# Twelve loads of small weights issued by GpSimd instead of SyncE, in a transformer block's forward and backward pass, with a new written-out order

## The chip, the cores and the metric

The kernel runs on one core of a Trainium2 chip. The metric is the device time of one execution in microseconds (us), as the median of several runs. A core has five engines with a queue of instructions each, and each queue is worked off in order: TensorE (PE; its weight loads are listed apart as PEld), VectorE (DVE), ScalarE (ACT), GpSimd (POOL) and SyncE (SP). SyncE only issues data movements (DMAs); ScalarE and GpSimd can issue them too. An instruction that waits for another engine, or for a DMA to land, holds up everything behind it in its own queue.

## The reference

The inputs are two batches of 4000 tokens with 144 channels, in bf16, and seven small weights. Shortened to what matters:

```python
xa = layernorm(x)
q, k, v = split(xa @ w_qkv)
glob = softmax(q @ k.T * D ** -0.5) @ v @ w_att_out
u, g = split(gelu(xa @ w_mlp_in))
g = layernorm(g)
loc = (u * conv5(g, dw_csgu)) @ w_mlp_out        # 5 taps along the tokens, per channel
m = concat(glob, loc)
out = x + (m + conv5(m, dw_merge)) @ w_merge
```

The kernel must return the output and, for a given grad_out, the gradients of x and of all seven weights.

## The kernel before

Tokens lie on 125 partitions, 32 blocks of 125 tokens to a batch. The body walks over the 64 blocks of both batches. For each block it computes the scores against all 4000 tokens of the batch (`ps`, four pieces of 1000; lines L1187 and L1194), the row minimum of the negated scores (L1209, on VectorE), the exponentials (L1215, on ScalarE, into `Pbuf`), the products for the backward pass (`Sbuf`), transposes of both by DMA (`PT`, `ST`), and the sums over tokens (L1236, L1266, L1322). Pieces of the local branch (the gelu and the convolution) are put between them. A last stage, from about 1000 us on, does the output and the weight gradients.

The head, the first 40 us, prepares this for batch 0. It does the following:

- It loads x in four groups of eight blocks, w_qkv, and the other weights. `Head.loads` (L148 to L163) issues w_qkv from ScalarE and the other twelve loads from SyncE. Each weight of 144 rows takes two loads, rows 0 to 127 (L153) and rows 128 to 143 (L154), into parts of the tile `raw`; `dwt` holds the merge taps (L157); `Wi` and `Wi2` hold w_mlp_in (L161 to L163).
- It computes the layernorm of x by groups: `lnst` (bn_stats on VectorE, L362), a few small steps to the variance `lnve` (L373), the root `rstd_x` (a power, on GpSimd, L374), `lnnm` (L378), then the normalized blocks `xa_aug`, two of a group on ScalarE (L383), four on VectorE (L385), two on GpSimd (L387). TensorE transposes them (L392 and L396), ScalarE copies the result to `xaT_m` (L393) and VectorE to `R` (L397); each group so has one R copy. A PSUM tile that an R copy reads is free for the next transposes only when the copy is done.
- It folds weights together: the q/k product `Q` and part of `RW` (L204, L205), the tap columns `cols` from transposes of `dwt` (L215, L217 to L219), the merge weight scaled by each tap (`sWm`: one half on ScalarE at L238, ten products; the other half on GpSimd at L240, ten products), the product of w_att_out with the value weights (L181) and from these `VUT` (L253, L259). `jit_q` and `jit_b` make the rows `qb` of the first two blocks, which TensorE transposes to `qt` (L1354).
- 36 matmuls on zeros (`warm`, L192) are spread over the head's TensorE queue.

The order within each queue is neither the program's order nor a scheduler's: the class `Planner` holds a table `ORDER` with one list of numbers for each of the five engines, over the whole program, and chains the instructions (on TensorE, runs of matmuls) in that order. The numbers count the instructions of an engine in program order, so a load that moves from one engine to another renumbers both lists.

Of the kernel before, what the change touches and what calls it, by code (L numbers as in the profile page):

```python
# [15 lines left out]
D = 144  # L16
DR = 16
# [103 lines left out]
class Head:  # L121
# [7 lines left out]
    def loads(self):  # L129
# [26 lines left out]
        ld(self.Wo, k.w_att_out, 0, nc.sync)  # L156
        nc.sync.dma_start(self.dwt[:], k.dw_merge)  # L157
        ld(self.Wl, k.w_mlp_out, 0, nc.sync)
        for h in range(2):
            ld(self.Wm[h], k.w_merge, h * D, nc.sync)  # L160
        nc.sync.dma_start(W.Wi[0:128, 0, :], k.w_mlp_in[0:128, :])  # L161
        nc.sync.dma_start(W.Wi[96:96 + DR, 1, :], k.w_mlp_in[128:D, :])
        nc.sync.dma_start(self.Wi2[:], k.w_mlp_in[128:D, :])  # L163
# [612 lines left out]
class Planner:  # L776

    ORDER = {
# [1414 lines left out]
```

## Time and profile before

| what | us |
|---|---|
| median of three runs | 1152.78 (1150.36 to 1153.01) |
| the profiled execution | 1152.39 |
| its span in the trace | 1150.5 |
| TensorE busy | 1118.8 (97%) |
| VectorE busy | 1021.0 (89%) |
| ScalarE busy | 906.5 (79%) |
| GpSimd busy | 249.5 (22%) |

The span runs from the first to the last instruction of the trace; the rest of the profiled execution's time lies around it. Views of the trace that the text uses: *stages* give each engine's busy time in stretches of the span; *waits* name who waited for whom; *the chain of waits* follows the last instruction back, at each step to what released it; *groups* add up the instructions of a line; *the timeline* lists them by start. "PE ps L1187" means an instruction of TensorE at line 1187 that writes the tile `ps`. A busy TensorE is modelled from pipelined matmuls, and the share of one engine over the whole span is a mean of stages with different limits.

### The profile page before, as it was taken

What the parts mean: (1) busy time and instruction counts of PE and PEld (TensorE: products, weight loads), DVE (VectorE), ACT (ScalarE), POOL (GpSimd) and SP (SyncE); (2) the same over time, 40 slices, a digit from 0 to 9 for tenths busy, and PEclk for the clock granted to TensorE, in tenths of its full rate; (3) what the DMA queues carried; (4) which work ended last, traced back from release to release, by engine and by line L of the source; (5) the groups of instructions that cost most, each with busy time, mean ns of one, the idle gap of its engine ahead of it and who ended that gap; (6) DMA issues with size and microseconds to landing.
All of it is one profiled execution on the core that took longest, in us unless ns stands there. A gap on an engine that the chain in (4) does not pass through costs nothing.

```text
span 1150.5 us, 35851 instructions
## 1 busy us (share of the span) xinstructions
PE 1118.8 (97%) x14293; PEld 868.7 (76%) x14293; DVE 1021.0 (89%) x3063; ACT 906.5 (79%) x1641; POOL 249.5 (22%) x427
## 2 busy tenths in 40 slices
PE   6999999999999999999999999999999999999998
PEld 3667777777777677777777777777777777699987
DVE  8699999999999998877999999999999997667656
ACT  5999898899898767777989889888889877615372
POOL 8111112111121113431001111111111112013642
PEclk9999999999999999999999999999999999999999
DMA  4688887979988989998988989888888899978973
GB/s 117 155 160 176 173 181 158 192 159 173 174 166 159 188 181 182 201 187 183 207 183 178 171 158 168 161 181 152 173 174 154 187 177 183 224 173 219 245 144 101
DMA packets 680887, 200.72 MB, mean 174 GB/s; under 512 B 657815, under 2 KB 674093, under 8 KB 680699
## 3 DMA queue, kind: packets, MB, share of 16 engines
q1 hardware_dynamic: 678352, 194.69, 84.6%
q0 software_dynamic: 2192, 3.62, 1.1%
q8 instruction: 111, 1.82, 0.7%
q14 instruction: 56, 0.46, 0.1%
q10 hardware_dynamic: 176, 0.12, 0.0%
HBM read 24.62 MB, written 18.01 MB: 37 GB/s over the span
## 4 chain that ended last, share of the span: by engine, by line
PE 64%; DMA 13%; DVE 11%; ACT 7%; issue 2%; SPq 1%; POOL 1%; ACTq 0%; DVEq 0%; POOLq 0%
PE X L1322 18%; PE ps L1187 14%; PE yz L1236 8%; PE yz L1266 8%; PE ps L1194 5%; DMA PT<-Pbuf 5%; DVE Pbuf L1209 4%; ACT Pbuf L1215 3%; PE po L1708 2%; DMA ST<-Sbuf 2%; PE pd L610 1%; DVE Sbuf L1226 1%; PE pj L1147 1%; ACT Sbuf L1225 1%; DMA go_h<-in_grad_out_dram 1%
## 5 line engine op out<-in xcount | busy, mean ns | idle before, releaser
L1209 DVE TENSOR_SCALAR_CACHE_REDUCE Pbuf<-ps 125x1000 bf16<-125x1000 f32 x256 | 306.2, 1197 | 30.1 <-PE ps L1194 22.4
L1225 ACT CAST Sbuf<-ps 125x1000 bf16<-125x1000 f32 x249 | 248.7, 999 | 86.7 <-PE ps L1194 66.2
L1215 ACT ACTIVATE Pbuf<-Pbuf,nm 125x1000 bf16<-125x1000 bf16 x256 | 284.9, 1144 | 4.4 <-DVE nm L1211 4.2
L1322 PE MATMUL X<-QBs,Pbuf 125*128 125x144 bf16 x2048 | 281.1, 226 | 0.2 <-POOL QBs L1256 0.2
L1322 PE MATMUL X<-QBs,Sbuf 125*128 125x144 bf16 x2048 | 281.3, 226 | 0.0
L1187 PE MATMUL ps<-xaT_m,qt 128*128 128x500 bf16 x1024 | 260.6, 374 | 5.0 <-DVE Pbuf L1209 3.5
L1322 PEld LDWEIGHTS <-Sbuf 125*128 125x128 bf16 x2048 | 198.2, 98 | 18.8 <-issue 18.5
L1322 PEld LDWEIGHTS <-Pbuf 125*128 125x128 bf16 x2048 | 200.2, 98 | 1.3 <-issue 1.1
L1226 DVE TENSOR_TENSOR Sbuf<-Sbuf,Pbuf 125x1024 bf16<-125x1024 bf16 x249 | 170.8, 690 | 7.9 <-ACT Sbuf L1225 6.0
L1236 PE MATMUL yz<-xa_aug,PT 125*128 125x145 bf16 x2048 | 151.0, 227 | 6.5 <-DMA PT<-Pbuf 6.4
L1266 PE MATMUL yz<-xa_aug,ST 125*128 125x144 bf16 x2048 | 150.8, 228 | 3.6 <-DMA ST<-Sbuf 2.4
L1236 PEld LDWEIGHTS <-PT 125*128 125x128 bf16 x2048 | 130.7, 98 | 21.6 <-DMA PT<-Pbuf 10.5
L1187 PEld LDWEIGHTS <-qt 128*128 128x128 bf16 x1024 | 91.4, 97 | 68.6 <-issue 7.0
L1266 PEld LDWEIGHTS <-ST 125*128 125x128 bf16 x2048 | 132.9, 98 | 12.2 <-issue 7.1
L1329 DVE TENSOR_TENSOR acc<-X,acc 125x432 f32<-125x432 f32 (+1 forms) x204 | 109.8, 548 | 15.3 <-PE X L1322 14.8
L1256 POOL TENSOR_TENSOR QBs<-g,g 125x144 bf16<-125x144 f32 x64 | 35.2, 550 | 379.2 <-ACT g L1255 290.9
L1194 PEld LDWEIGHTS <-qt 16*128 16x128 bf16 x1024 | 26.3, 91 | 108.9 <-issue 108.9
L1194 PE MATMUL ps<-XR,qt 16*128 16x500 bf16 x1016 | 100.4, 380 | 0.0
L681 POOL TENSOR_SCALAR l_w<-ring,nc,c 125x144 f32<-125x144 bf16 x64 | 31.8, 504 | 167.0 <-DVE nc L677 122.4
L653 DVE TENSOR_TENSOR l_prod<-ring,Wc 125x720 bf16<-125x720 bf16 x128 | 65.9, 535 | 0.2
L1611 PE MATMUL Hps<-Yg,go_h 125*128 125x144 bf16 x640 | 54.3, 226 | 0.0
L600 POOL TENSOR_TENSOR rsr<-ve,mhalf 125x2 f32<-125x2 f32 x32 | 25.4, 795 | 126.9 <-DVE ve L599 107.4
(540 smaller groups left out, 1946.4 us busy)
## 6 DMA issues: line engine op xcount, KB each, us to landing
Yn_d<-yn SPq DMA_DIRECT2D x64, 36.0 KB
Zn_d<-qb SPq DMA_DIRECT2D x64, 36.0 KB
ug_d<-ugr SPq DMA_DIRECT2D x32, 72.0 KB
Yg<-Yn_d SPq DMA_DIRECT2D x8, 288.0 KB
Yg<-ug_d SPq DMA_DIRECT2D x8, 288.0 KB
Zn<-Zn_d SPq DMA_DIRECT2D x4, 576.0 KB
PT<-Pbuf SPq DMA_TRANSPOSE x128
ST<-Sbuf SPq DMA_TRANSPOSE x128
```

The lines of the kernel that those rows point to most:

```text
L653: nc.vector.tensor_tensor(prod[:, bi].rearrange("p a b -> p (a b)"), ring[:, a, p + bi:p + bi + 5, :].rearrange("p a b -> p (a b)"), W.Wc[ ...
L1187: mm = nc.tensor.matmul(pp[r // 2][:, r % 2, 0:CH], QT[i][:, 2 * h, :], bs(i)[0].xaT_m[:, c * CH:(c + 1) * CH], start=True, stop=False)
L1194: nc.tensor.matmul(pp[r // 2][:, r % 2, 0:CH], QT[i][rs, 2 * h + 1, :], xr, start=False, stop=True)
L1209: nc.vector.tensor_scalar(pv(pc(i, c2)), src, -1.0, 3.0e38, op0=ALU.mult, op1=ALU.min, accum_out=NM[i][:, c2:c2 + 1])
L1215: nc.scalar.activation(v, v, ACT.Exp, bias=NM[i][:, 4:5], scale=-1.0)
L1225: nc.scalar.copy(pv(sc(i, c2)), src)
L1226: nc.vector.tensor_tensor(sc(i, c2), sc(i, c2), pc(i, c2), op=ALU.mult)
L1236: nc.tensor.matmul(Yw, PT[0:PB, pos(i, j), :], S.xa_aug[:, j, 0:D + 1], start=(j == 0), stop=(j == NB - 1))
L1266: nc.tensor.matmul(Zw, ST[0:PB, j, :], S.xa_aug[:, j, 0:D], start=(j == 0), stop=(j == NB - 1))
L1322: nc.tensor.matmul(X[:, jj, :], l, r, start=(n_ == 0), stop=(n_ == len(ops) - 1))
L1329: nc.vector.tensor_tensor(av, X[0:PB, 0:nj, :], av, op=ALU.add)
L1611: nc.tensor.matmul(H[0:rows, a // 3, (a % 3) * D:(a % 3 + 1) * D], lhs, self.src[b][h][:, 2 + j, :], start=(n == 0 and a % 3 == 0), stop=( ...
```

## The change

The twelve loads other than w_qkv are issued by GpSimd. In the program they stand in another order: the taps first, then the two halves of w_merge (the second half first), then w_att_out, w_mlp_out and w_mlp_in. SyncE is left with x, grad_out, the zeros that fill the pads, and what comes later. All five lists of `ORDER` are new, over the whole program and not only in the head. No instruction computes anything else than before. Lines behind the edit have a number higher by 1 (from L158 of the old on), behind the table by 2.

```diff
         ld(self.Wqkv, k.w_qkv, 0)
-        ld(self.Wo, k.w_att_out, 0, nc.sync)
-        nc.sync.dma_start(self.dwt[:], k.dw_merge)
-        ld(self.Wl, k.w_mlp_out, 0, nc.sync)
-        for h in range(2):
-            ld(self.Wm[h], k.w_merge, h * D, nc.sync)
-        nc.sync.dma_start(W.Wi[0:128, 0, :], k.w_mlp_in[0:128, :])
-        nc.sync.dma_start(W.Wi[96:96 + DR, 1, :], k.w_mlp_in[128:D, :])
-        nc.sync.dma_start(self.Wi2[:], k.w_mlp_in[128:D, :])
+        e = nc.gpsimd
+        e.dma_start(self.dwt[:], k.dw_merge)
+        for h in (1, 0):
+            ld(self.Wm[h], k.w_merge, h * D, e)
+        ld(self.Wo, k.w_att_out, 0, e)
+        ld(self.Wl, k.w_mlp_out, 0, e)
+        e.dma_start(W.Wi[0:128, 0, :], k.w_mlp_in[0:128, :])
+        e.dma_start(W.Wi[96:96 + DR, 1, :], k.w_mlp_in[128:D, :])
+        e.dma_start(self.Wi2[:], k.w_mlp_in[128:D, :])
...
     ORDER = {
-        "PE": [36, 37, 38, 39, 40, 41, 0, 1, 42, 2, 3, 4, 5, 43, 6, 7, 8, 44, 9, 10, 11, 53, 12, 45, 13, 46, 14, 47, 15, 16, 17, 48, 18, 54, 19, 49,
+        "PE": [36, 37, 38, 39, 40, 41, 0, 42, 1, 2, 3, 4, 5, 6, 43, 7, 8, 9, 44, 10, 11, 12, 53, 13, 45, 14, 46, 15, 16, 47, 17, 18, 54, 19, 48, 20,
```

GpSimd's queue behind the first rstd, before:

```order
L387 TENSOR_SCALAR xa_aug_114<-Sbuf,rstd_x_65,lnnm_101 125x144
L374 TENSOR_TENSOR rstd_x_65<-lnve_100,mhalf 125x8
L1119 MEMSET Pbuf 125x144x3
L387 TENSOR_SCALAR xa_aug_114<-Sbuf,rstd_x_65,lnnm_101 125x144 x2
L374 TENSOR_TENSOR rstd_x_65<-lnve_100,mhalf 125x8
L2024 MEMSET A_dwc 128x240
L387 TENSOR_SCALAR xa_aug_114<-Sbuf,rstd_x_65,lnnm_101 125x144 x2
L374 TENSOR_TENSOR rstd_x_65<-lnve_100,mhalf 125x8
L65 MEMSET go_q_95 29x288
L535 DMA held_1_924<-zdram 16x36
L387 TENSOR_SCALAR xa_aug_114<-Sbuf,rstd_x_65,lnnm_101 125x144 x2
L240 TENSOR_SCALAR sWm_310<-raw,cols 128x144 x2
```

The same stretch now:

```order
L154 DMA raw<-in_w_merge_dram 16x144
L1132 MEMSET qb_129 128x768
L375 TENSOR_TENSOR rstd_x_65<-lnve_100,mhalf 125x8
L154 DMA raw<-in_w_att_out_dram 16x144
L388 TENSOR_SCALAR xa_aug_114<-Sbuf,rstd_x_65,lnnm_101 125x144
L1121 MEMSET Pbuf 125x144x3
L388 TENSOR_SCALAR xa_aug_114<-Sbuf,rstd_x_65,lnnm_101 125x144
L375 TENSOR_TENSOR rstd_x_65<-lnve_100,mhalf 125x8 x2
L388 TENSOR_SCALAR xa_aug_114<-Sbuf,rstd_x_65,lnnm_101 125x144 x4
L153 DMA raw<-in_w_att_out_dram 128x144
L154 DMA raw<-in_w_mlp_out_dram 16x144
L241 TENSOR_SCALAR sWm_310<-raw,cols 128x144
```

Of the twelve loads, dwt is the first entry of GpSimd's head, and three of 128 rows (both halves of w_merge and w_mlp_out) stand with memsets ahead of the first rstd; five stand among the rstd and the normalizations (four of them shown, the fifth, of 16 rows of w_merge, just ahead of the rows shown), and the three of w_mlp_in behind the tap products. The last two rstd follow each other, and the last four normalizations follow both. Three qb memsets stood ahead of the first rstd and now one does; the `sr` products, the `Wc` copy, `held` and other memsets went behind the tap products.

ScalarE's queue behind the first four copies from PSUM (`two`), before:

```order
L205 ACTIVATE RW<-hps 16x144
L205 ACTIVATE Q_283<-hps 128x144
L383 ACTIVATE xa_aug_114<-Sbuf,lnnm_101,rstd_x_65 125x144 x2
L217 CAST cols<-hps 128x2x5
L393 COPY xaT_m_118<-pt 128x1000
L238 ACTIVATE sWm_309<-raw,cols 128x144 x2
```

And now:

```order
L218 CAST cols<-hps 128x2x5
L219 CAST cols<-hps 16x2x5
L239 ACTIVATE sWm_309<-raw,cols 128x144
L220 ACTIVATE cols<-cols 128x4
L206 ACTIVATE RW<-hps 16x144
L384 ACTIVATE xa_aug_114<-Sbuf,lnnm_101,rstd_x_65 125x144 x2
L206 ACTIVATE Q_283<-hps 128x144
L239 ACTIVATE sWm_309<-raw,cols 128x144
```

The tap columns and the first tap product moved ahead of the normalizations of the first group.

VectorE's queue around the second R copy, before:

```order
L1209 TENSOR_SCALAR Pbuf,nm<-ps 125x8x125
L385 TENSOR_SCALAR xa_aug_114<-Sbuf,rstd_x_65,lnnm_101 125x144
L397 COPY R_119<-pt 16x1000
L385 TENSOR_SCALAR xa_aug_114<-Sbuf,rstd_x_65,lnnm_101 125x144 x3
L378 SCALAR_TENSOR_TENSOR lnnm_101<-lnsm_99,rstd_x_65 125x8
L385 TENSOR_SCALAR xa_aug_114<-Sbuf,rstd_x_65,lnnm_101 125x144 x4
L397 COPY R_119<-pt 16x1000
L1209 TENSOR_SCALAR Pbuf,nm<-ps 125x8x125
```

And now:

```order
L386 TENSOR_SCALAR xa_aug_114<-Sbuf,rstd_x_65,lnnm_101 125x144 x4
L398 COPY R_119<-pt 16x1000
L379 SCALAR_TENSOR_TENSOR lnnm_101<-lnsm_99,rstd_x_65 125x8
L386 TENSOR_SCALAR xa_aug_114<-Sbuf,rstd_x_65,lnnm_101 125x144
L1211 TENSOR_SCALAR Pbuf,nm<-ps 125x8x125
L386 TENSOR_SCALAR xa_aug_114<-Sbuf,rstd_x_65,lnnm_101 125x144 x3
L398 COPY R_119<-pt 16x1000
L1211 TENSOR_SCALAR Pbuf,nm<-ps 125x8x125
```

The first row minimum (L1209, now L1211) moved behind the second R copy, and three normalizations ahead of it. Ahead of the first R copy there are now 22 bn_stats in place of 24. On TensorE, one of the two warm matmuls between the first two groups of transposes (L392, L396) moved behind them, and the four score matmuls that stood behind the transposes of the second block's qb (L1354) now stand ahead of these.

More of the change, by code (lines that the diff above doesn't have):

```diff
@@ L778 @@
     ORDER = {
[53 rows of a table removed]
-        "DVE": [0, 2, 1, 3, 4, 10, 5, 11, 9, 8, 6, 7, 12, 14, 15, 13, 16, 17, 40, 43, 25, 18, 44, 20, 22, 23, 19, 32, 24, 21, 34, 33, 35, 36, 26, 28,
[102 rows of a table removed]
-        "Activation": [1, 0, 4, 5, 2, 3, 7, 6, 8, 9, 10, 13, 29, 32, 14, 15, 11, 33, 16, 17, 18, 12, 37, 35, 34, 19, 20, 21, 24, 22, 23, 31, 27, 26,
[64 rows of a table removed]
-        "Pool": [8, 5, 15, 4, 11, 0, 12, 10, 1, 3, 47, 7, 2, 16, 18, 6, 19, 17, 41, 25, 26, 24, 50, 33, 32, 31, 9, 53, 37, 38, 20, 30, 42, 23, 13,
[44 rows of a table removed]
[53 rows of a table added]
+        "DVE": [0, 1, 2, 3, 4, 5, 9, 8, 11, 10, 7, 6, 12, 14, 15, 16, 13, 17, 22, 19, 18, 20, 25, 42, 23, 41, 24, 32, 21, 34, 33, 44, 35, 36, 26, 28,
[102 rows of a table added]
+        "Activation": [1, 0, 2, 3, 4, 5, 10, 11, 29, 12, 7, 8, 9, 6, 33, 13, 14, 15, 35, 32, 16, 17, 18, 31, 19, 23, 24, 30, 20, 21, 36, 26, 22, 27,
[64 rows of a table added]
+        "Pool": [7, 0, 8, 20, 22, 14, 19, 6, 27, 1, 10, 4, 2, 28, 9, 30, 31, 11, 23, 29, 13, 37, 53, 38, 36, 43, 44, 45, 50, 49, 12, 15, 32, 3, 42,
[45 rows of a table added]
     }
```

519 rows, old and new, of the table ORDER are left out of this document.

## The prediction

> **What bounds the kernel now.** I read the stages first, then what TensorE waits for, then the chain of waits through the head, then the rows of the engines around it. The stages (us; each engine's busy time and count, granted clock, DMA share, GB/s):
>
> ```profile
> 0.00:40.00 40.00, 29.70 (x278) 19.44 (x278) 30.60 (x105) 26.52 (x65) 25.38 (x55) 1.00 0.52 128
> 40.00:60.00 20.00, 19.69 (x190) 12.49 (x189) 13.32 (x24) 19.02 (x47) 1.54 (x3) 1.00 0.68 164
> 60.00:1000.00 940.00, 924.96 (x11577) 699.14 (x11575) 877.81 (x2538) 791.97 (x1386) 164.77 (x275) 1.00 0.90 176
> 1000.00:1100.00 100.00, 99.23 (x1583) 97.25 (x1582) 68.22 (x266) 43.62 (x76) 40.90 (x72) 1.00 0.91 213
> 1100.00:1150.50 50.50, 45.25 (x676) 40.36 (x673) 31.01 (x133) 25.40 (x71) 16.96 (x23) 0.98 0.48 114
> ```
>
> The first number after the length is TensorE (PE). From 40 us on it is busy nearly all the time; it is free 10.3 us of the first 40, where the edited loads are, and 15.0 us of the 940 behind them. So a head that ends earlier moves all that follows by as much, and the new order behind the head can give back no more than those waits. Nearly all of the 15.0 us are these (what waits, for whom: total, times, longest):
>
> ```profile
> PE yz L1236 <- DMA PT<-Pbuf: 6.4, 11, 1.0
> PE ps L1187 <- DVE Pbuf L1209: 3.3, 11, 0.9
> PE yz L1266 <- DMA ST<-Sbuf: 2.4, 3, 1.2
> PE ps L1187 <- DMA qt<-qb: 1.0, 2, 0.5
> ```
>
> The chain of waits in the head (start, length, what):
>
> ```profile
> 1.91 4.34 DMA raw<-in_w_qkv_dram
> ...
> 7.43 3.08 DMA dwt<-in_dw_merge_dram
> ...
> 11.05 0.95 PE pt L392 x8
> 12.01 0.43 PE warm L192 x2
> 12.43 0.85 PE pt L396 x8
> ...
> 18.18 1.21 DVE Pbuf L1209 x2
> ...
> 19.65 0.70 DVE R L397
> ...
> 20.77 0.42 PE ps L1187 x2
> 21.20 0.53 PE ps L1194 x2
> 21.72 0.22 PE warm L192
> ...
> 28.60 2.11 ACT Pbuf L1215 x2
> ...
> 36.92 0.22 PE pj L1360
> ```
>
> The tap load, issued only at 7.43, holds TensorE; then TensorE until 13.3, VectorE until 20.4, TensorE, ScalarE from 28.0 to 36.7, and TensorE from there. These rows of the timeline carry the rest (in brackets: the engine's idle time before, and who ended it):
>
> ```profile
> 7.13 1.99 DVE L362 BATCH_NORM_STATS2 lnst<-Sbuf 125x6 f32<-125x144 bf16 x9 [0.37 <-DMA Sbuf<-in_x_dram]
> 9.67 0.89 ACT L383 ACTIVATE xa_aug<-Sbuf,lnnm,rstd_x 125x144 bf16<-125x144 bf16 x2
> 10.56 0.50 PE L215 MATMUL hps<-ident,dwt 5*128 5x5 bf16 x4 [1.41 <-DMA dwt<-in_dw_merge_dram]
> 11.15 0.17 ACT L217 CAST cols<-hps 128x10 f32<-128x10 bf16 x1 [0.59 <-PE hps L215]
> 12.93 0.72 ACT L238 ACTIVATE sWm<-raw,cols 128x144 bf16<-128x144 bf16 x2
> 13.31 0.69 DVE L397 COPY R<-pt 16x1000 bf16<-16x1000 bf16 x1 [1.20 <-PE pt L396]
> 20.37 0.77 DVE L385 TENSOR_SCALAR xa_aug<-Sbuf,rstd_x,lnnm 125x144 bf16<-125x144 bf16 x3
> 20.98 0.74 POOL L535 DMA_DIRECT2D held<-zdram  x1
> 22.97 0.69 DVE L397 COPY R<-pt 16x1000 bf16<-16x1000 bf16 x1 [0.72 <-PE pt L396]
> 25.74 0.29 PE L181 MATMUL hps<-two,raw 128*128 128x144 bf16 x2
> 27.12 1.20 DVE L1209 TENSOR_SCALAR_CACHE_REDUCE Pbuf<-ps 125x1000 bf16<-125x1000 f32 x1 [0.19 <-PE ps L1194]
> ```
>
> **The change part by part.** *Twelve issues on GpSimd.* The same weights are loaded from GpSimd at the end of this kernel, which gives the price: the issue, and the time from it to landing (min/median/max). GpSimd's work in the head is priced by its groups:
>
> ```profile
> L105 POOL DMA_DIRECT2D RW<-in_w_merge_dram x1: 602/602/602, 1093.6 to 1093.6; - x1
> DMA to landing us min/median/max: 2.7/3.0/4.7
> ...
> L374 POOL TENSOR_TENSOR rstd_x<-lnve,mhalf 125x8 f32<-125x8 f32 x4 | 6.6, 1654 | 2.4 <-DVE lnve L373 1.5 <-DMA Sbuf<-in_x_dram 0.9
> L387 POOL TENSOR_SCALAR xa_aug<-Sbuf,rstd_x,lnnm 125x144 bf16<-125x144 bf16 x8 | 3.8, 486 | 2.0 <-DVE lnnm L378 1.0 <-DVE lndm L371 0.9
> L1130 POOL MEMSET qb<- 128x768 bf16 x3 | 2.1, 730 | 0.0
> ```
>
> An issue costs 0.60 us (the row of 0.74 in the timeline is the upper end), twelve 7.2 to 8.9. Four stand ahead of the first rstd; two qb memsets of 0.73 and three weight memsets went behind, and GpSimd had waited 0.9 there, so I take no delay (bounds 0 and 0.6). The load that GpSimd issues latest for an early use is w_att_out: behind it in its queue stand the ten tap products, ahead of it all four rstd, all eight normalizations, one qb and three issues. From 6.85, when the first rstd begins, that is 6.6 + 3.8 + 0.73 + 3 x 0.60 = 12.9 us of work. GpSimd's waits there are 2.4 + 2.0, less the 0.9 ahead of 6.85, so 3.5; issues and the memset fill 2.5 of them. The load is issued at 6.85 + 12.9 + 1.0 + 0.7 (the Pbuf memset, taken as long as a qb one) = 21.5, and lands at 24.5 by the median, 26.2 at worst. TensorE uses it at 25.74 in the old run. It is in time by the median, but only by about half a microsecond once the head is earlier: this wait may take the place of the one removed.
>
> *SyncE loses twelve issues.* None of the waits above is on a load of its queue except dwt and the first x. Price nothing. What costs is the company: three GpSimd loads (two of 37 KB, one of 3 KB) now share the DMA engines with w_qkv and the first x before 6 us. At the 128 GB/s of the first row they last 0.6 us. Bounds 0 and 0.6; I take a loss of 0.2, since w_qkv's own queue goes on beside them.
>
> *The tap wait.* dwt is first in GpSimd's queue and lands within the first 6 us even at 4.7 us. The 1.41 us go. What is late next: ScalarE's two normalizations, which end at 10.56 in the old run and feed the transposes of 11.05. But ScalarE now does three tap-column steps (0.17 each) and one tap product (0.36) ahead of them, 0.87 us, and they end near 11.4. Its product needs the other half of w_merge, the fourth GpSimd issue, some 3.7 us after the first (its memsets in between), so landed by 9.2 at worst, when ScalarE gets there near 9.7, where its normalizations began. With the second half of the transposes (0.95 / 2) behind it the first group ends at 11.9, against 12.00: 0.1 gained. One of two warm-up matmuls between the groups is moved away (0.21, of which I take half). Together **0.2** (bounds 0 and 0.7, the latter if the normalizations were not delayed).
>
> *The order on VectorE.* Of its bn_stats two (1.99 / 9 = 0.22 each) move behind the R copy of 13.31, where it had waited 1.20: that costs the path **0.44**. Against that its first row minimum (1.21) moves behind the second R copy and three normalizations (0.77) ahead of it, so the second R copy comes as long after the first as now (0.44 + 0.77 - 1.21 = 0). Behind it VectorE waited 0.72 for transposes and 0.19 for scores. TensorE now does the scores of 20.77 to 21.94 (1.17 us) ahead of the transposes that wait for the second R copy, so the second group's transposes come earlier by as much, and both waits go: **0.91** (bounds 0.2 and 1.0). What is late next is VectorE itself, busy up to the last row minimum, and ScalarE behind it, whose exponentials and copies up to 36.9 keep their number.
>
> *The new order behind 40 us.* All lists change; counted in the two PE lists, 596 of 1385 numbers stand at another place. The instructions are the same. The rows show no sign for the sum of the shifts: zero, with the waits of TensorE as the measure.
>
> The sum: 0.2 + 0.91 - 0.44 - 0.2 = 0.5 us less. The profiled execution took 1152.4, the median of the three runs is 1152.8; from this the forecast is **1152.3**. About 0.3%, 3.5 us, is what a measurement of this kernel can tell from no change, so the forecast is "same".
>
> A rule speaks against GpSimd as issuer. The Trainium skill, SBUF — State Buffer, section "SBUF: two separate sides", says that a GpSimd DMA's descriptors can't be written while VectorE runs an operation in a two-port mode, and that one of about 620 ns then takes about 3100. By it, four issues (three plus the w_att_out load) would cost an estimated 4 x 2.5 = 10 us, the landing would be near 34.5 and the kernel would end near 1161.5, against 1152.3 by the rows. The trace doesn't agree so far: the issue at 20.98 ran beside VectorE's normalizations of 20.37 to 21.14 and took 0.74, though no row here shows one beside a copy.
>
> **The rivals.** (1) *The order behind the head gains.* The four waits add to 13.1 us. If the new order avoids half of them, the time is 1152.3 - 6.5 = 1145.8; it counts as faster from about 3 us. For it: the waits come in 27 pieces, up to 1.2 us each, that a shift of one place can undo. Against it: with every list shifted, an order that undoes one wait can make another, and no row shows which.
>
> (2) *It loses there*, by the same measure: half as much again, 1158.8.
>
> (3) *GpSimd is late, and TensorE stands at the w_att_out product.* In the old run the load lay on SyncE and TensorE came there at 25.74. Now every microsecond that GpSimd loses between 6.85 and 21.5 passes to the landing at 24.5; beyond 25.74 the kernel is later one for one. If each of the four issues is held for one row minimum of VectorE (1.20), the landing is at 29.3 and the time 1152.8 + 29.3 - 25.74 = 1156.4. It decides against the 0.3% from 4.7 us of delay on. For it: GpSimd's queue is the densest of the head. Against it: the 0.74 row. The SBUF page's rule above is what would bring it.
>
> (4) *The wait for dwt becomes a wait of the same length for ScalarE*: within the forecast's bounds, 1152.8 to 1153.4.
>
> **How the numbers follow.** Forecast with (4): 0.55. Rival 1: 0.24. Rival 2: 0.13. Rival 3: 0.08. So faster 0.24, same 0.55, slower 0.21. The range goes from 1147 (about half of rival 1 left out, 0.12) to 1157 (about 0.08 of rival 2 left out, rival 3 inside); the forecast's own range is 1149.5 to 1155.5.
>
> **What would show it.** Right: no wait of TensorE for dwt; a first R copy near 13.1; no wait ahead of the third R copy; the row minima of the first tile ended near 27.6, not 28.3; the jit_b product of 36.92 about 0.5 earlier; TensorE's free time from 60 to 1000 us near 15. Wrong: a wait of TensorE for raw near 25 (rival 3), GpSimd issues in the head of over 1 us, ScalarE waiting for w_merge, or a free time between 60 and 1000 that differs by over 3 us (rivals 1 and 2).

## The result: 0.9% slower, and the loss is in the last stage

| kernel | median, us | runs | ratio to before, 95% interval |
|---|---|---|---|
| before | 1152.77 | 1150.36 to 1153.01 (4) | |
| after | 1160.59 | 1159.08 to 1165.11 (4) | 1.0086, 1.0059 to 1.0112 |

The ratio isn't the quotient of the two medians, which is 1.0068; in either form the kernel after is slower by 8 to 10 us. The forecast was 1152.3 and "same", with a range from 1147 to 1157. The profiled execution of the kernel after took 1160.08 us, its span is 1158.3. These are its stages (us; TensorE's busy time is the first number behind the length), cut more finely behind 1000 us than in the prediction:

```profile
0.00:40.00 40.00, 30.26 (x278) 19.77 (x278) 32.20 (x105) 26.62 (x65) 31.31 (x66) 1.00 0.51 125
40.00:1000.00 960.00, 944.00 (x11743) 712.98 (x11742) 887.16 (x2556) 810.99 (x1432) 165.36 (x278) 1.00 0.88 175
1000.00:1060.00 60.00, 59.20 (x931) 57.30 (x929) 37.27 (x132) 23.94 (x39) 12.35 (x25) 1.00 0.85 204
1060.00:1100.00 40.00, 34.38 (x544) 33.95 (x542) 30.08 (x115) 16.24 (x30) 23.96 (x38) 1.00 1.02 219
1100.00:1158.30 58.30, 52.56 (x810) 48.09 (x807) 34.65 (x160) 28.67 (x77) 21.86 (x32) 0.98 0.46 119
```

And the same cut of the kernel before, where it differs from the rows shown:

```profile
40.00:1000.00 960.00, 944.65 (x11764) 711.63 (x11763) 891.13 (x2561) 810.99 (x1432) 166.31 (x278) 1.00 0.90 176
1000.00:1060.00 60.00, 59.68 (x942) 58.08 (x941) 38.40 (x140) 24.92 (x42) 13.79 (x28) 1.00 0.82 197
1060.00:1100.00 40.00, 39.55 (x645) 39.17 (x643) 29.82 (x129) 18.70 (x35) 27.10 (x45) 1.00 1.03 238
```

TensorE's free time (length less busy) went from 10.3 to 9.7 us in the head, 15.35 to 16.0 up to 1000, 0.3 to 0.8 up to 1060, **0.45 to 5.6 from 1060 to 1100**, and 5.25 to 5.7 behind. Together that is 6.2 us more. Its busy time grew by 1.6 us (sums 1118.8 and 1120.4): the clock fell once in the loop, near 593 (the rows are in the last section). 6.2 + 1.6 = 7.8 is the whole difference of the spans.

What TensorE waits for now (total, times, longest):

```profile
PE yz L1268 <- DMA ST<-Sbuf: 5.8, 5, 1.7
PE yz L1238 <- DMA PT<-Pbuf: 3.6, 7, 1.1
PE po L1710 <- DVE xo L1713: 2.7, 2, 1.9
PE Hps L1613 <- DMA Yg<-ug_d: 2.0, 1, 2.0
PE pm L1536 <- DVE xo L1713: 1.0, 1, 1.0
```

The last three are new or grew; `po` waited 0.4 before. Here is the stretch of the last stage in which they lie, by the timelines of TensorE, VectorE and GpSimd:

```profile
1082.08 0.60 PE L1613 MATMUL Hps<-Yg,go_h 125*128 125x144 bf16 x7 [1.97 <-DMA Yg<-ug_d]
1089.09 0.47 PE L1710 MATMUL po<-VUl,goT 128*125 128x144 bf16 x5 [1.91 <-DVE xo L1713]
1098.16 0.60 PE L1536 MATMUL pm<-ident,Yr 125*128 125x125 bf16 x8 [0.97 <-DVE xo L1713]
...
1082.03 1.99 DVE L1736 SCALAR_TENSOR_TENSOR t<-xa_aug,dx_s,acc 125x144 f32<-125x144 bf16 x1 [3.97 <-POOL dxo L1739]
1088.60 0.81 DVE L1713 TENSOR_TENSOR xo<-po,xo 125x288 bf16<-125x288 f32 x2
1095.24 0.37 DVE L1736 SCALAR_TENSOR_TENSOR t<-xa0r,dx_s,acc 125x144 f32<-125x144 bf16 x1 [4.94 <-POOL dxo L1739]
...
1080.73 1.26 POOL L1739 TENSOR_TENSOR dxo<-t,go_h 125x576 bf16<-125x576 f32 x1 [4.06 <-DMA out_dram<-dxo]
1093.31 0.66 POOL L1598 COPY Yr<-Yg 125x576 bf16<-125x576 bf16 x1 [3.00 <-DMA Yg<-ug_d]
```

VectorE makes two things here: `t`, a step of the gradient of x, which GpSimd adds up into `dxo`, and `xo`, which takes a finished `po` out of PSUM. A new `t` waits until `dxo` has read an old one, and GpSimd's `dxo` waits for a store or stands behind the `Yr` copies, which wait for `Yg`. So VectorE stands 3.97 and 4.94 us at a `t`; the `xo` behind it come late, and TensorE has no free `po`.

The head neither gained nor lost: the jit_b product of 36.92 stands at 36.90. Its rows (TensorE, VectorE, GpSimd, SyncE):

```profile
36.90 0.22 PE L1362 MATMUL pj<-RW,R 128*125 128x144 bf16 x1 [0.16 <-ACT M1T L183]
...
9.69 0.53 DVE L386 TENSOR_SCALAR xa_aug<-Sbuf,rstd_x,lnnm 125x144 bf16<-125x144 bf16 x2
10.35 1.57 DVE L386 TENSOR_SCALAR xa_aug<-Sbuf,rstd_x,lnnm 125x144 bf16<-125x144 bf16 x2
13.36 0.69 DVE L398 COPY R<-pt 16x1000 bf16<-16x1000 bf16 x1 [0.42 <-PE pt L397]
...
10.56 0.55 POOL L154 DMA_DIRECT2D raw<-in_w_merge_dram  x1
11.11 0.76 POOL L1132 MEMSET qb<- 128x768 bf16 x1
...
4.82 0.36 SPq L2022 DMA_DIRECT2D zdram<-zt  x1
```

Two normalizations of VectorE that took 0.53 took 1.57 beside GpSimd's issue and memset, and ended (11.92) when the memset ended (11.87).

### The profile page after: what moved, and what is told of

Its sections match the earlier page's. It is cut to its first block, busy times and chain, and to the rows that moved or that the text cites. A ratio compares the mean times of both kernels' runs of the same rounds, so it can differ in the third digit from the quotient of the medians.

```text
span 1158.3 us, 35824 instructions
## 1 busy us (share of the span) xinstructions
PE 1120.4 (97%) x14293; PEld 872.1 (75%) x14293; DVE 1021.3 (88%) x3063; ACT 906.5 (78%) x1641; POOL 254.8 (22%) x439
## 4 chain that ended last, share of the span: by engine, by line
PE 69%; DVE 13%; DMA 8%; ACT 6%; issue 3%; POOL 1%; SPq 0%; DVEq 0%; ACTq 0%; POOLq 0%
PE X L1324 18%; PE ps L1189 14%; PE yz L1238 9%; PE yz L1268 8%; PE ps L1196 5%; DVE Pbuf L1211 4%; DMA PT<-Pbuf 3%; PE Hps L1613 3%; PE po L1710 3%; ACT Pbuf L1217 2%; DMA ST<-Sbuf 2%; PE pd L611 1%; DVE Sbuf L1228 1%; PE pj L1149 1%; DMA Yg<-ug_d 1%
## 5 line engine op out<-in xcount | busy, mean ns | idle before, releaser
L1211 DVE TENSOR_SCALAR_CACHE_REDUCE Pbuf<-ps 125x1000 bf16<-125x1000 f32 x256 | 305.9, 1196 | 28.6 <-PE ps L1196 23.0
L1737 ACT ACTIVATE t<-t,dx_c,rstd_x 125x144 f32<-125x144 f32 x64 | 28.7, 499 | 29.5 <-DVE t L1736 15.9
```

Source lines behind the costliest of these rows:

```text
L1211: nc.vector.tensor_scalar(pv(pc(i, c2)), src, -1.0, 3.0e38, op0=ALU.mult, op1=ALU.min, accum_out=NM[i][:, c2:c2 + 1])
```

## The experiments

The two programs issue the same instructions (twelve loads from another engine), so an order can be put together from both: "the order of A up to a product, then that of B" means the instructions that A's program puts ahead of that product, in A's order, and then all others in B's. Four stretches are told apart: the head (up to the first yz product), the loop (up to the first Hps product, about 1013 us), the last stage, and in it the part from the first po product on (about 1060). Every row is 5 to 12 runs beside the kernel before on the same chip (e5 one run, without a ratio). Since the median of before moved between 1148.8 and 1151.9 from chip to chip, the ratios are compared.

| run | what it is | median | ratio, interval |
|---|---|---|---|
| e1 | new head, old order behind | 1152.29 | 1.0003, 0.9988 to 1.0018 |
| e2 | new last stage alone | 1155.92 | 1.0042, 1.0027 to 1.0058 |
| e3 | new loop alone | 1161.69 | 1.0075, 1.0050 to 1.0100 |
| e4 | loads on GpSimd, old order | 1156.62 | 1.0046, 1.0027 to 1.0064 |
| e6 | e2, dxo first | 1151.76 | 1.0011, 0.9999 to 1.0022 |
| e7 | e1, head mended | 1149.93 | 0.9995, 0.9980 to 1.0011 |
| e8 | e3, ST first | 1158.83 | 1.0076, 1.0052 to 1.0099 |
| e9 | after again | 1159.58 | 1.0079, 1.0059 to 1.0099 |
| e10 | after, ST first | 1160.36 | 1.0080, 1.0061 to 1.0098 |
| e11 | after, dxo first | 1159.89 | 1.0085, 1.0060 to 1.0109 |
| e12 | after, ST, dxo and head | 1156.80 | 1.0066, 1.0042 to 1.0089 |
| e13 | after, pads first | 1162.75 | 1.0098, 1.0066 to 1.0130 |
| e14 | after, old order from first po on | 1153.42 | 1.0023, 1.0008 to 1.0037 |
| e15 | e12, pads first | 1157.81 | 1.0068, 1.0044 to 1.0093 |
| e16 | e14, ST and head | 1153.09 | 1.0022, 1.0007 to 1.0037 |
| e17 | after, SyncE old from first po on | 1159.93 | 1.0090, 1.0067 to 1.0113 |
| e18 | e17, GpSimd old too | 1158.99 | 1.0088, 1.0067 to 1.0109 |

**Which stretch (e1 to e4).**

```diff
 e1 (program of after), all five lists of ORDER
-  after's to the end
+  after's up to the first yz product, before's behind it
 e2, e3 (program of before), all five lists
-  before's to the end
+  e2: before's up to the first Hps product, after's behind it
+  e3: before's in head and last stage, after's in the loop
 e4 (program of after)
-  after's order
+  before's order; only GpSimd's head, with the twelve loads, is after's
```

> The kernel after with its own order up to the first yz product (about 36 us), and behind that every engine in the order of the kernel before. The twelve loads are on GpSimd. Theory A (the loss is made by the new order of the last stage and a part by that of the loop; the head gives and costs nothing, since the jit_b product stands at 36.90 after and 36.92 before): 1152.8, within 1.5. Theory B (the loads on GpSimd cost, by what they do to the DMA queues or to VectorE, whatever the order behind them): near 1160.6, and TensorE's free time behind 40 us as in the kernel after.

> The kernel before, its twelve loads on SyncE and its order up to the first Hps product (about 1013 us), and behind that every engine in the order of the kernel after. Theory A: the last po product came 6.4 us later after than before and the loop's end 2.1 us later, so the last stage is worth 4.3, and with the 1.4 us between the last po product and the end 5.7: 1152.8 + 5.7 = 1158.5, with VectorE waiting for GpSimd's dxo (about 9 us in the two longest) and TensorE for xo. Theory B: 1152.8.

> The kernel before in its head and in its last stage; between the first yz product and the first Hps product every engine in the order of the kernel after. The twelve loads are on SyncE. Theory A: the loop's end was 2.1 us later after than before, so 1152.8 + 2.1 = 1154.9. Theory C (the order of the loop alone shifts what meets in the last stage, and the whole loss follows): near 1160. Theory B: 1152.8.

> The twelve loads on GpSimd, its head queue that of the kernel after; every other engine, and GpSimd behind the head, in the order of the kernel before. Theory A: the issuer alone is worth at most the microsecond or so that VectorE stands beside GpSimd's work in the head, less the tap wait of 1.41: 1152.8, from 1151.5 to 1154.5. Theory B: near 1160.6.

e1 bears theory A out: with the twelve loads on GpSimd and the new head the kernel is as fast as before, so it isn't the loads that cost 8 us, whatever they do to queues or ports. e2 lost 4.0 where 5.7 was expected. e4 missed A's forecast, and B's too. It is some 5 us slower than before (0.46%), nearly all of it in the head, where its jit_b product stands at 41.63 instead of 36.92:

```profile
32.65 0.39 PE L1196 MATMUL ps<-XR,qt 16*128 16x500 bf16 x2 [2.72 <-DMA XR<-R]
41.63 0.22 PE L1362 MATMUL pj<-RW,R 128*125 128x144 bf16 x1 [0.21 <-ACT M1T L183]
```

The rows of SyncE show where this comes from, and it isn't the issuing of the twelve loads:

```profile
28.82 2.41 SPq L400 DMA_DIRECT2D XR<-R  x4
```

```profile
SPq L336 <- POOL go_q L65: 10.3, 1, 10.3
```

The first row is the timeline's, the other is a wait of SyncE in the first 40 us. In GpSimd's new list a memset of `go_q` (L65) stands behind the tap products; it runs from 27.74 to 28.07. SyncE's old list has a load into `go_q` that waits for this memset, and behind that load the four loads of `XR`. So SyncE stands 10.3 us at one memset (2.4 before) and issues `XR` at 28.82 instead of 23.69. TensorE waits 2.72 for it, and behind that wait its clock is at half for some 3.4 us, which costs another 1.7: together 4.4 of the 4.7 us. e4 shows what the new list of one engine costs beside the old lists of the others. The issuer alone is priced by no run.

e3 lost more than any theory but C gave, and the trace (its shortest run, 1154.8) didn't show where. e5 is the same kernel once more, and e8 takes away the one long wait of that trace by an edit on SyncE:

```diff
 e8, SyncE near 588 us (line numbers of before)
+L1405 DMA_TRANSPOSE ST<-Sbuf 128x16x128
 L53 DMA ring<-ring 112x2x288
 L48 DMA acc_d<-acc 13x1152
 L53 DMA ring<-ring 12x2x288
-L1405 DMA_TRANSPOSE ST<-Sbuf 128x16x128
```

> The kernel with the new order of the loop alone, once more, for the trace of an execution near its median (it took 1154.8 to 1164.1, and the one profiled so far was the shortest). If the loop's order loses through waits for ST (1.85 us at 593 in the first trace) and through the clock behind them (0.5 for some 3.4 us behind a wait of 1.71 at 593 in the kernel after, so 1.7 us more), an execution of 1161 shows three or four such pairs of 3 to 4 us. If it loses elsewhere, TensorE's waits for ST add to no more than the 4.4 us of the first trace.

> The kernel with the new order of the loop alone, and on SyncE one transpose of ST (issued at 588.7, behind two stores of ring and one of acc, the last of which waits for VectorE until 588.5) moved ahead of these three. If this wait makes the loop's loss: TensorE's wait of 1.85 at 593 goes, and with it the clock's fall behind it, 2 to 5 us of the 8.6 to 9.8: 1157 to 1160. If many waits make it together: 1160 to 1162.

e5 took 1160.56. Its waits for ST add to 6.3 us, the longest is 1.61, and the clock falls behind none of them, so the three or four pairs of the expectation aren't there. The timeline of TensorE in e5:

```profile
595.12 1.19 PE L1266 MATMUL yz<-xa_aug,ST 125*128 125x144 bf16 x16 [1.61 <-DMA ST<-Sbuf]
1023.42 1.19 PE L1236 MATMUL yz<-xa_aug,PT 125*128 125x145 bf16 x16 [2.96 <-DMA PT<-Pbuf]
```

And in e8:

```profile
1018.09 2.13 PE L1236 MATMUL yz<-xa_aug,PT 125*128 125x145 bf16 x16 [4.09 <-DMA PT<-Pbuf]
```

The edit did what it should, the wait near 593 is gone. But both traces stand 3 to 4 us for a PT near 1020, where the new loop meets the old last stage. The short run of e3 has only 0.23 there, and the kernel after has no such wait (its waits for PT from 990 us on are 0.57 at most). So e3 and e8 overstate the loop: their seam costs. e14, which has its seam later, is the better measure.

**The head's standstill (e7).**

```diff
 GpSimd's head
-L1132 MEMSET qb_129 128x768
 L375 TENSOR_TENSOR rstd_x_65<-lnve_100,mhalf 125x8
+L1132 MEMSET qb_129 128x768
 SyncE's head
-L2022 DMA zdram<-zt 128x128
 L43 DMA Sbuf<-in_x_dram 13x1152
+L2022 DMA zdram<-zt 128x128
```

> The kernel with the new head and the old order behind it (1152.3), with two edits in the head: SyncE issues the store of zeros (zdram), which waits for a memset of GpSimd until 4.8, behind the last x load of 13 rows instead of ahead of it; GpSimd clears the second qb behind the second rstd instead of ahead of it. Theory H1 (these two hold VectorE, which the head's chain follows: 0.51 us waiting for x and about 1.1 in a normalization that takes 1.57 instead of 0.53): the normalization takes 0.55, the second R copy ends 1.2 to 1.6 earlier than 20.5 to 20.9, and the time is 1151, from 1150.5 to 1152. Rival H2 (the issue of a load on GpSimd at the same moment holds VectorE, not the memset): the normalization still takes about 1.1, ended by the issue's end, and the gain is 0.4 to 0.9. Rival H3 (ScalarE or TensorE is late next): VectorE is earlier, the jit_b product isn't.

```profile
10.20 0.53 DVE L386 TENSOR_SCALAR xa_aug<-Sbuf,rstd_x,lnnm 125x144 bf16<-125x144 bf16 x2
...
10.41 0.54 POOL L154 DMA_DIRECT2D raw<-in_w_merge_dram  x1
...
36.24 0.22 PE L1362 MATMUL pj<-RW,R 128*125 128x144 bf16 x1 [0.16 <-ACT M1T L183]
```

H2 falls: beside the same issue (10.41 to 10.95), with no memset behind it, the normalizations take 0.53. So it took the memset to hold VectorE, as H1 has it. The first R copy begins at 12.70 instead of 13.36. The jit_b product is 0.66 earlier than after, about half of what H1 gave: the x load was issued 1.05 earlier (4.17), but VectorE went on with it only 0.14 earlier. The time, 0.9995, can't be told from before.

**What the last stage loses (e6, e9 to e13, e15).** The edits on GpSimd, in the last stage:

```diff
 dxo first (e6, e11, e12, e15)
+L1739 TENSOR_TENSOR dxo<-t_19847,go_h_19352 125x576
+L48 DMA out_dram<-dxo 13x576
 L1598 COPY Yr_20449<-Yg_19985 125x576
 L1760 MEMSET WoT 128x144
+L1739 TENSOR_TENSOR dxo<-t_19916,go_h_19352 125x576
 L1598 COPY Yr_20451<-Yg_19988 125x576
-L1739 TENSOR_TENSOR dxo<-t_19847,go_h_19352 125x576
-L48 DMA out_dram<-dxo 13x576
-L1739 TENSOR_TENSOR dxo<-t_19916,go_h_19352 125x576
 pads first (e13, e15)
+L65 MEMSET Yg_19985 29x288
+L65 MEMSET Yg_19988 29x288
 L1739 TENSOR_TENSOR dxo<-t_19571,go_h_19352 125x576
 L1631 MEMSET ym_19311 32x1024
 L1739 TENSOR_TENSOR dxo<-t_19640,go_h_19352 125x576
-L65 MEMSET Yg_19988 29x288
-L65 MEMSET Yg_19985 29x288
```

> The kernel with the new order of the last stage alone, and on GpSimd two dxo additions (and one store behind the first) moved ahead of the two Yr copies. Theory A1 (the copies wait 4.0 and 2.8 us for Yg, dxo stands behind them, VectorE's t waits 6.2 for dxo, xo stands behind t, and TensorE's po and pm behind xo): the waits of 1.64 and 0.95 on TensorE go, 1155.9 - 2.6 = 1153.3, and VectorE's longest wait for dxo falls to below 3. Rival A2 (the loads on SyncE's queue are what is late, and the copies only show it): TensorE waits for Yg or Yr instead, 1155.9.

> The kernel after once more, beside the next three on the same chip: 1.0086 of before, 1.0059 to 1.0112; its trace should show the same waits of TensorE as the first (ST 1.71 near 593; Yg 1.97, xo 1.91 and 0.77, pm 0.97 in the last stage), with lengths that differ by up to a microsecond.

> The kernel after with one edit on SyncE: the transpose of ST near 588 ahead of the two stores of ring and one of acc. Theory: the wait of 1.71 at 593 goes, and where the clock fell behind it, another 1.7: 1.7 to 3.4 less than the kernel after. Rival (the wait only moves to the next transposes): the same as after.

> The kernel after with one edit on GpSimd: two dxo additions and one store ahead of the two Yr copies. Theory A1: TensorE's waits for xo (1.91, 0.77, 0.97) go or shrink, 3 to 4 us less than the kernel after, as it was worth in the kernel with the new last stage alone. Rival A2 (the loads on SyncE's queue are late; the wait of 1.97 for Yg is untouched): at most 1 us less.

> The kernel after with the three edits together: ST first, dxo first, and the head's two (the store of zeros behind the last x load, the second qb cleared behind the second rstd; worth 0.66 at the jit_b product). If these are what the new order lost: 1160.6 - 3.4 - 3.7 - 0.7 = 1152.8, no slower than the kernel before; and below it, if the new order gains where nothing holds it up (row minima near 940 stood 1.7 to 5.8 us earlier than before). If the loss has more sources: 1155 to 1158.

> The kernel after with one edit on GpSimd: the two memsets of the pads of Yg ahead of the two dxo additions (which wait 2.1 to 4.3 us for a store) instead of behind them. Theory P (SyncE's queue stands 3.7 to 3.9 us for these pads in every trace of this order, and with it the loads of Yg, xo and xa0r behind it): SyncE's wait goes, TensorE's waits for Yg, xo and xa0r (5 to 7 us together) fall by half or more, 1156 to 1157, 1.005 of before. Rival Q (the loads take 5 to 7 us each there whoever issues them when, and come late by that): the waits stay, 1.008.

> The kernel after with all edits together: ST first, dxo first, the head's two, and the pads first. The four without the pads gave 1.0066, with one trace whose last row minimum was 3.2 us earlier than before and whose last stage lost it again. Theory P: 0.998 to 1.002. Rival Q: 1.006.

In e6 the edit was worth what theory A1 gave: 1.0042 became 1.0011. Its trace, a long run (1158.64), doesn't show A1's way to it: VectorE's longest wait for dxo is 5.5 there and not below 3, and TensorE waits 3.20 for an xo. e9, the kernel after again, has the waits of the first trace with other lengths (ST 0.75 near 593, Yg 1.54, xo 2.71, pm 0.87). In the kernel after it was worth nothing (e11), nor was ST first (e10), nor the pads (e13). In each the wait that was aimed at is gone, and another is as long. The timeline of TensorE in e10, which has no wait near 593 any more:

```profile
441.96 1.19 PE L1268 MATMUL yz<-xa_aug,ST 125*128 125x144 bf16 x16 [2.24 <-DMA ST<-Sbuf]
1069.52 1.16 PE L1683 MATMUL pz<-xa0r,Zn 125*128 125x144 bf16 x16 [1.80 <-DMA xa0r<-xa_d]
1089.97 0.47 PE L1710 MATMUL po<-VUl,goT 128*125 128x144 bf16 x5 [2.58 <-DVE xo L1713]
```

In e11 the wait for xo is gone, and that for Yg is 2.64:

```profile
1082.73 0.60 PE L1613 MATMUL Hps<-Yg,go_h 125*128 125x144 bf16 x7 [2.64 <-DMA Yg<-ug_d]
```

And in e13, whose SyncE no longer stands for the pads, VectorE stands 12.1 us at a `t` for dxo (in the other traces of this order up to 7.2), and TensorE 7.59:

```profile
1097.34 0.76 PE L1710 MATMUL po<-VUl,goT 128*125 128x144 bf16 x5 [7.59 <-DVE xo L1713]
```

Theories A1 and P are wrong as the cause in the kernel after; Q fits, and e12 and e15 came out in their second cases (more sources, and Q): the last row minimum of e12's trace came 3.2 us earlier than in the kernel before, and its last stage lost that again. What fills a gap there are loads and transposes, in e12's chain of waits:

```profile
1069.37 5.01 DMA Yg<-ug_d
...
1075.55 6.72 DMA YT<-ym
...
1086.98 6.91 DMA xa0r<-xa_d
```

Their length alone doesn't set the kernels apart: the chain of the kernel before has pieces as long between 1060 and 1100 us (7.65 at a store of dxo, 5.54 at a transpose into goT), and TensorE is busy there. Why dxo first mends e2 and not the kernel after stays open.

**Which part of the last stage, and whose order (e14, e16, e17, e18).**

```diff
 program of after, ORDER from the first po product on
-  after's
+  e14, e16: before's, all five lists (e16 with the edits of e7 and e8 as well)
+  e17: before's on SyncE alone
+  e18: before's on SyncE and GpSimd
```

> The kernel after up to its first po product (about 1060 us), and behind that every engine in the order of the kernel before. Theory A (the order from there on makes most of the loss; the traces lose 5 to 7 us between the last row minimum and the end): 1154.5 to 1156, 1.003 to 1.005 of before. Theory C (the loss is made ahead of it, in the loop): 1.008.

> The kernel after with ST first and the head's two edits, and from the first po product on the order of the kernel before. If the loop's new order gains about 3 us where ST holds nothing up (the last row minimum 2.6 and 3.2 us earlier in two traces) and the old last stage costs what it cost before: 1147 to 1149, 0.997 to 0.999. If the old last stage loses where it meets the new loop (a late PT near 1020 in two traces): 1.002 to 1.006.

> The kernel after, and from its first po product on SyncE alone in the order of the kernel before. Theory S (the loss is the order of the loads and transposes on SyncE: Yg behind a waiting transpose, xo and xa0r late): 1.002 to 1.004 of before. Theory V (it is the order of the work on the other four, and the loads only show it): 1.008.

> The same with GpSimd too in the order of the kernel before from there on. Theory S: 1.002 to 1.004, as e17. A third theory, G (GpSimd's order, dxo behind the Yr copies and the pads, makes it): e17 1.008 and this 1.002 to 1.004. Theory V: 1.008 for both.

The old order from the first po product on takes the kernel from 1.0079 to 1.0086 down to 1.0023: of a loss of 0.79 to 0.86%, 0.56 to 0.63 are made there. With SyncE's order alone, or SyncE's and GpSimd's, nothing comes back; theories S and G fall, and V is left: the order of TensorE, VectorE and ScalarE in the last stage makes the loss. This is argued and not shown. The old order of these three beside the new one of the other two wasn't run, and e4 showed that a mix of lists can cost 4.7 us of its own. Nor is the order of the three enough: e6 has it, behind the old loop and with dxo first, and is at 1.0011. One stretch tells the kernels apart, the row from 1060 to 1100 us. With the old order there, the lowest of nine traces (e1), and e14:

```profile
1060.00:1100.00 40.00, 37.98 (x613) 37.56 (x615) 26.63 (x113) 14.89 (x30) 23.41 (x39) 1.00 0.94 213
```

```profile
1060.00:1100.00 40.00, 39.64 (x647) 39.43 (x645) 30.45 (x129) 16.04 (x31) 25.52 (x41) 1.00 0.99 237
```

With the new order of the three engines, the highest of eleven (e2), and e17:

```profile
1060.00:1100.00 40.00, 36.43 (x577) 36.04 (x576) 31.74 (x118) 19.71 (x38) 23.24 (x36) 1.00 0.99 221
```

```profile
1060.00:1100.00 40.00, 33.00 (x481) 32.61 (x479) 25.10 (x94) 14.82 (x28) 22.41 (x35) 0.91 0.96 234
```

TensorE is busy 38.0 to 40.0 of the 40 us with the old order and 29.0 (e13) to 36.4 with the new, and no trace lies between. VectorE's wait for dxo divides them the same way, though by little at the border: 7.6 to 13.7 us (e1) with the old order, 14.0 (e6) to 27.6 with the new. The traces at the border, of e1 and e6, are long runs of kernels whose medians are those of the kernel before. The rows of e14 and of e17 (from 1050 us on):

```profile
DVE t L1736 <- POOL dxo L1739: 8.0, 3, 3.8
```

```profile
DVE t L1736 <- POOL dxo L1739: 25.6, 7, 7.1
```

VectorE's own list fits: of its 32 `xo`, the eleventh and the twelfth stand behind 24 `t` in the old list and behind 31 in the new, the fifteenth behind 35 and 40; up to the tenth the two lists differ by 3 at most. An `xo` with seven more `t` ahead of it stands for every `dxo` that these wait for. That VectorE's list and not TensorE's or ScalarE's makes it is argued from these rows; the three weren't tried apart.

e16, put together from what gained, isn't faster than the kernel before: no version here is, by more than a measurement can tell.

## Why the prediction was wrong, point by point

*The twelve issues: right.* The price was 0.60; the issues of the head take 0.50 to 0.65. The first rstd began at 7.10, 0.25 later than before, where no delay was taken, and within the bound of 0.6. It came behind a memset of `two` in GpSimd's queue (until 6.98) and behind a small step of VectorE that this memset held (until 7.01; see the last section). The 128-row load of w_att_out was issued at 22.06 (21.5 forecast), and TensorE's product didn't wait for it. Rival 3 didn't come.

*The rule of the Trainium skill* (SBUF — State Buffer, "SBUF: two separate sides"), by which the issues would have cost 10 us: they didn't. No issue took over 0.65, and of the loads into `raw` and `dwt` none landed later than 4.5 us behind its issue. The hold went the other way here: VectorE's normalization lasted as long as GpSimd's memset. The page has it that the one of the two that starts first keeps the port. By the rows the normalization (the second of its pair, from 10.57) began ahead of the memset (11.11) and was held all the same, so they don't bear this out.

*SyncE, "price nothing": wrong, but small.* SyncE's store of zeros waits for a memset, which now stands behind GpSimd's issues (4.82 instead of 3.97), and the 13 rows of x stand behind that store. VectorE waits 0.51 for x at 8.54. With the 13 rows issued 1.05 earlier (e7) it went on only 0.14 earlier, so most of that wait has another cause. Work taken from a queue can still make it wait, by what the queue waits for.

*The tap wait: right.* It is gone, and ScalarE's normalizations end at 11.2 (11.4 forecast). The first R copy is at 13.36, not near 13.1: the memset beside VectorE (1.57 instead of 0.53) took what the tap wait gave. With that memset moved away and the load of x earlier (e7) it is at 12.70, and the jit_b product 0.66 earlier. No term of the sum has this hold.

*VectorE's order in the head: the waits went, the time didn't.* The third R copy waits no more, as forecast. But the last row minimum of the tile, which was to end 0.5 to 0.7 earlier, begins at 27.12 in both kernels, with the first R copy at 13.31 before and 13.36 after. So 0.05 was gained and not 0.91 - 0.44 = 0.47. What took the rest isn't shown.

*"The new order behind 40 us: the rows show no sign for the sum of the shifts: zero, with the waits of TensorE as the measure": this is the step that failed.* From 60 to 1000 us it nearly held: TensorE was busy 924.62 there, 924.96 before, though 1.6 us of the 924.62 are what the fall of the clock at 593 cost. The loss lies from 1060 to 1100, where TensorE was free 0.45 of 40 us. The measure was the 13.1 us that TensorE waited, nearly all in the loop: that is what a new order can give back. What it can lose isn't bounded by it. A stretch without waits has nothing to gain and everything to lose, and here four engines stand in a ring (TensorE's po, VectorE's xo behind t, GpSimd's dxo, ScalarE's t) with loads and transposes that take 5 to 7 us. The lists said where to look: a number of VectorE's list stands 7.4 places away on average in the last tenth, 2.3 to 3.9 in the others.

*Rival 2* had the size (1158.8), but not the place, and its chance of 0.13 was too small. Its sign to look for, a free time from 60 to 1000 that differs by 3 us, didn't appear.

The loop's share stays rough. e14 has the new head and the new loop and is 1.0023 (1.0008 to 1.0037), so about 2.6 us, while the loop alone gave 1.0075 with its seam.

## What to carry to other kernels

The waits in a trace price what a new order can give, and say nothing of what it can take: look for the stretch with the least slack and the most engines in a ring, and read there how many steps now stand ahead of each one that another engine waits for. When a single wait is taken away and the time stays, look at the stretch's busy time and not at the next wait: only putting a whole stretch back, then single queues of it, showed where the loss was, and whose order alone it wasn't. A mix of two orders has costs of its own (e4, one memset; e5 and e8, a seam), so what a mix loses is first looked up in its trace and not put down to either order.

## What the runs showed of the hardware

**A wait of TensorE can cost more than its length.** The clock over the wait of 1.71 us at 593 in the kernel after (the clock granted is the third number from the end):

```profile
591.00:593.00 2.00, 0.39 (x5) 0.10 (x4) 1.93 (x6) 2.00 (x5) 0.49 (x1) 1.00 1.10 308
593.00:595.00 2.00, 1.90 (x17) 1.91 (x18) 1.52 (x4) 2.00 (x3) 0.00 (x0) 0.55 0.75 186
595.00:597.00 2.00, 2.00 (x22) 2.00 (x20) 1.47 (x4) 1.58 (x4) 0.00 (x0) 0.60 1.28 105
597.00:599.00 2.00, 2.00 (x30) 1.77 (x28) 0.29 (x1) 0.00 (x0) 0.00 (x0) 1.00 1.25 278
```

Behind the wait the clock is at half for about 3.4 us, which costs 2 x 0.45 + 2 x 0.40 = 1.7 us more, as much as the wait. In the twenty traces TensorE waited 49 times for 1.2 us or longer behind the head. All 8 waits of 2.64 us or more had such a fall in them or behind them, and 5 of the 41 shorter ones, the shortest of 1.38 (e6, at 438), while one of 2.60 (e14, at 441) had none. What divides them is in the traces too. The falls of one trace lie whole multiples of 3.41 us apart (e15: 440.27 and 1085.39, which is 189 times). Cut the time between the head and the last 8 us into stretches of 3.41 us on that grid: behind each of the 11 at full clock in which TensorE was free for 1.87 us or more (about half) the clock fell, behind two of the eleven with 1.59 to 1.85 us, and behind no other. The wait of 2.60 lies across two stretches, with 1.57 and 1.03. The Trainium skill, TensorE: Matmul & The Clock Gate, section "What's actually happening", gives an idle window of about 3.4 us, which runs freely, as what brings the half clock; here less than half of that was enough once. The runs of one kernel differ by up to 11 us (e13), and the clock is a part of it: the mean clock was 0.997 in its shortest run and 0.994 in its longest, which is some 3.5 us.

**GpSimd's memsets and additions can hold VectorE**; an issue alone didn't. In the head of the kernel after a small step of VectorE and a normalization lasted as long as a memset:

```profile
6.42 0.59 DVE L374 TENSOR_SCALAR lnve<-lnve 125x8 f32<-125x8 f32 x1
...
10.57 1.35 DVE L386 TENSOR_SCALAR xa_aug<-Sbuf,rstd_x,lnnm 125x144 bf16<-125x144 bf16 x1
```

The first ends with the memset of `two` (6.02 to 6.98). In the fourteen traces with GpSimd's new head it takes 0.45 to 0.73, in the six with the old head, where no memset runs then, 0.17. The second ends with the memset of `qb` (11.87), and takes 0.31 without it (e7). In the last stage a `t` takes 1.99 us from 1082.03 on, beside a `dxo` addition (1082.55 to 1083.84), where its neighbours take 0.36.
